# Recurrent-memory attention in a pipelined pair of layers: first step written out with segment 0's values made in place, and one-layer steps with another order and another output projection

## The chip, the core and the metric

The kernel runs on one core of one Trainium2 chip. The core has a matrix engine (TensorE, PE in the profile, with its weight loads as PEld), a vector engine (VectorE, DVE), an activation engine (ScalarE, ACT), GpSimd (POOL), a queue engine that only issues transfers (SyncE, SP), and 16 DMA engines that move data between DRAM and the on-chip memory SBUF. Matrix products are accumulated in PSUM, whose banks are read by DVE and ACT. The metric is the device time of one execution in microseconds (us); lower is better. Times are compared by their median.

## The reference

Four layers follow each other on a sequence of 2048 tokens of width 512 in bf16: attention with a recurrent memory (A), a dense block (B), A again, B again, each behind a layer norm and with a residual. Weights are shared by the two A layers and by the two B layers.

```python
def _A_ref(x, mem0, Wq, Wk, Wv, Wo, seg_len):       # M=8 memory rows, segments of 32 tokens, H=32 heads of 128
    mem = mem0
    for s in range(n_seg):                          # 64 segments, one after the other
        h = jnp.concatenate([mem, xs], axis=1)      # 40 rows: memory, then the segment's tokens
        q, k, v = h @ Wq, h @ Wk, h @ Wv            # per head
        p = softmax(mask(q @ k.T * scale))
        o = (p @ v) @ Wo
        mem = o[:, :M]                              # the memory of the next segment
        outs.append(o[:, M:])
x = x + _A_ref(_layernorm(x), ...); x = x + relu(_layernorm(x) @ w1) @ w2   # w1 512x1376, w2 1376x512
x = x + _A_ref(_layernorm(x), ...); x = x + relu(_layernorm(x) @ w1) @ w2
```

## The kernel before

**Steps.** Segment s+1 needs the memory that segment s leaves, so each A layer is a chain of 64 links. The kernel runs the second A layer four segments behind the first: step k works on segment k of the first layer and segment k-4 of the second. Steps 4 to 63 have both layers; steps 0 to 3 and 64 to 67 have one (`layers(k)` has one entry). The dense block of a position is done two steps later and fills gaps of the chain.

**Order.** PE, DVE, SP and POOL execute in the order in which the code is written. Only ACT's order is chosen by a planner, by priority; `tc.high_priority` marks the work of the chain.

**One step, `step(k)`**, in PE's order: queries and keys of heads 0 to 15 (`qk(0)`, three batches, products L466, copies L470 on ACT and L472 on DVE); the first part of the previous step's token projection (`block`, which calls `output_x(k-1)`, L349 for 32 rows, L328 for 64); `scores` (L496) and `softmax` (L512 to L526); `qk(1)` for heads 16 to 31; hidden layer of the dense block (`dense_h`, L408, ReLU on ACT L411); scores and softmax of heads 16 to 31; the rest of `block`; `dense_y` (L426); `transpose_p(1)` (L534, copies L538); weighted values (`weighted_v`, L560) and their copies (`outputs`, L578); the projection of the memory rows (`output_mem`, L504); its copy `wm` (ACT L740); values of the second layer's next tokens (`values1`, L309); `mt`, which turns `wm` (L753), and its copies to `HT` (DVE L758, memory rows for the next queries and keys) and to `HTm` (ACT L759, memory rows for the next values); `memory_values(k+1)` (L638). `HT` and `HTm` open the next step.

**On DVE** the add of the token projection into the residual, `add_output(k-1)` (L363), is written between the softmax of heads 16 to 31 and `transpose_p(1)`; the add of the dense block, `add_dense` (L334), after `outputs`. Then come `HT`, the norm's moments, the norm and the masks.

**Probabilities** of heads 0 to 15 are transposed by a DMA (`turn_p`, L541, from `P_sb` to `PT0`), except in steps 0, 1 and 67 (`by_pe`), where PE does it. The softmax of heads 16 to 31 writes the same `P_sb`, so it waits for that DMA.

**Values** go through DRAM. `values0(p, n)` makes the first layer's values of two segments (64 tokens; L288) and stores them in `vd0[p]` (L297); `memory_values` makes those of the memory rows and of some later tokens and stores them in `vmd` (L643); `load_values` (L614 to L622) and `load_memory_values` (L648) bring them to `Vs`, whose rows are keys. In step 0 these stores and loads are issued by POOL (`q = nc.gpsimd`), in later steps by SP.

**Banks.** `ps_c` has three PSUM banks (tag "c"), `ps_fill` two, `ps_wo` one. `output_x` and `output_mem` both use `ps_wo`, so `output_mem(k)` cannot start before `add_output(k-1)` has read the bank. SBUF tiles of tag "vst" (five) stage what is stored to DRAM.

**Start.** SP issues the weights in the order Wq, Wk (first halves), Wv, second halves of Wq and Wk, then Wo in four quarters; the dense weights w1 and w2 come in step 1 (`load_dense`, L151 to L154).

Of the kernel before, what the change touches and what calls it, by code (L numbers as in the profile page):

```python
# [7 lines left out]
BF = mybir.dt.bfloat16  # L8
# [14 lines left out]
def kernel(  # L23
# [254 lines left out]
    def values0(p, n, lo=0, hi=NC4, pool=None):  # L278
        r = 64 * (p % 2)
        if (n, lo) == (0, 0):  # L280
            vd0[p] = dram.tile([64, H * Dh], BF, tag="vd0", bufs=3, name="vd0")
        if lo == 0:
            pool, tag = (pool, "wo") if pool else (ps_fill, "fill")
            vp_tiles[p, n] = pool.tile([128, 512], F32, tag=tag, name="vp")
        vp = vp_tiles[p, n]
        for c4 in range(lo, hi):
            for j in range(2):
                nc.tensor.matmul(vp[64 * j:64 * j + 64, :], lhsT=xT0[p // 2][:, c4, r:r + 64],  # L288
                                 rhs=Wv_sb[:, c4, (n + j) * 512:(n + j + 1) * 512],
                                 start=(c4 == 0), stop=(c4 == NC4 - 1), tile_position=(0, 64 * j))  # L290
        if hi < NC4:
            return
        q = nc.sync if p >= 1 else nc.gpsimd
        vst = wk.tile([128, 512], BF, tag="vst", bufs=5)
        nc.scalar.copy(out=vst[:], in_=vp[:])
        for j in range(2):
            q.dma_start(out=vd0[p][:, (n + j) * 512:(n + j + 1) * 512], in_=vst[64 * j:64 * j + 64, :])  # L297

    def values1(s, ii):
        if not has1(s):  # L300
            return
        if ii == 0:
            vd1[s] = dram.tile([2, 4, 32, 512], BF, tag="vd1", bufs=3, name="vd1")
        r = base(s - DELTA)
        vp = ps_fill.tile([128, 512], F32, tag="fill", name="v1")
        for c4 in range(NC4):
            for j in range(4):
                n = 4 * ii + j
                nc.tensor.matmul(vp[32 * j:32 * j + 32, :], lhsT=xnT_tiles[s - 1][:, c4, r:r + SEG],  # L309
                                 rhs=Wv_sb[:, c4, n * 512:(n + 1) * 512],  # L310
                                 start=(c4 == 0), stop=(c4 == NC4 - 1), tile_position=(0, 32 * j))
        vst = wk.tile([128, 512], BF, tag="vst", bufs=5)
        nc.scalar.copy(out=vst[:], in_=vp[:])
        nc.sync.dma_start(out=vd1[s][ii].rearrange("j t e -> (j t) e"), in_=vst[:])
# [22 lines left out]
    def output_x(k, lo, hi):  # L337
        if not 0 <= k <= LAST or ox_span(k) is None:
            return
        r0, r1 = [x % 64 for x in (ox_span(k)[0], ox_span(k)[1] - 1)]  # L340
        r1 += 1
        if lo == 0:
            wo_tiles[k] = ps_wo.tile([128, Dm], F32, tag="wo", name="wox")
        for h in range(lo, hi):
            if r1 - r0 == 64:
                halves(wo_tiles[k], OTx[:, h, r0:r1], Wo_sb[:, h, :], h == 0, h == H - 1)
            else:
                for j in range(4):
                    nc.tensor.matmul(wo_tiles[k][32 * j:32 * j + 32, 0:128], lhsT=OTx[:, h, r0:r1],  # L349
                                     rhs=Wo_sb[:, h, 128 * j:128 * j + 128], start=(h == 0), stop=(h == H - 1),  # L350
                                     tile_position=(0, 32 * j))

    def add_output(k):
        if not 0 <= k <= LAST or ox_span(k) is None:
            return
        r0, r1 = ox_span(k)
        R = residual(k)
        if r1 - r0 == 64:
            add_halves(R[r0:r1, :], R[r0:r1, :], wo_tiles[k])
        else:  # L360
            for j in range(4):
                cs = slice(128 * j, 128 * j + 128)
                nc.vector.tensor_tensor(out=R[r0:r1, cs], in0=R[r0:r1, cs],  # L363
                                        in1=wo_tiles[k][32 * j:32 * j + 32, 0:128], op=ALU.add)
# [246 lines left out]
    def load_values(k, act, q):  # L611
        for a in act:
            if a == 1:
                q.dma_start(out=Vs[64 + M:64 + L, :].rearrange("t (n e) -> t n e", n=NCH),  # L614
                            in_=vd1.pop(k)[:].rearrange("i j t e -> t (i j) e"))
            elif k >= 4 and k % 4 < 2:
                for u in range(2):
                    lo = M + 2 * M * u
                    q.dma_start(out=Vs[lo:lo + 2 * M, :].rearrange("t (n e) -> t n e", n=NCH),
                                in_=vmds[k - k % 4 - 4 + 2 * (k % 4) + u][:, :, 2 * M:32, :].rearrange("i j t e -> t (i j) e"))  # L620
            else:
                q.dma_start(out=Vs[M:L, :], in_=vd0[k // 2][SEG * (k % 2):SEG * (k % 2) + SEG, :])  # L622
# [8 lines left out]
    def memory_values(k, q):  # L631
        vmd = vmds[k] = dram.tile([2, 4, 32, 512], BF, tag="vmd", bufs=7, name="vmd")
        for ii in range(2):
# [7 lines left out]
            VmS = wk.tile([128, 512], BF, tag="vst", bufs=5, name="VmS")  # L641
            nc.scalar.copy(out=VmS[:], in_=vp[:])  # L642
            q.dma_start(out=vmd[ii].rearrange("j t e -> (j t) e"), in_=VmS[:])  # L643

    def load_memory_values(k, act, q):
        for ii in range(2):
            for a in act:
                q.dma_start(out=Vs[64 * a:64 * a + M, 2048 * ii:2048 * (ii + 1)].rearrange("m (j e) -> m j e", j=4),  # L648
                            in_=vmds[k][ii, :, a * M:(a + 1) * M, :].rearrange("j t e -> t j e"))
# [12 lines left out]

    def step(k):
        act = layers(k)
        q = nc.sync if k > 0 else nc.gpsimd
# [3 lines left out]
        by_pe = k in (0, 1, LAST)  # L669
        if k % 4 == 0 and has_x:  # L670
            load_xb(n_x)
        if k == 0:
            masks(*act)
        with tc.high_priority(offset=PRIO):
            qks = qk(0, act)
        if k == 0:
            for n in range(0, NCH, 2):
                values0(0, n)
        with tc.high_priority(offset=PRIO):
            if k == 1:  # L680
                load_values(k, act, q)
            if k < 2:
                memory_values(k, q)
            if k != 1:
                load_values(k, act, q)
        part = 5 if len(act) == 2 else 8
        block(k, 0, part)
        with tc.high_priority(offset=PRIO):
            transpose_step(k)
            load_memory_values(k, act, q)  # L690
            scores(qks, act)
            softmax(0, act, by_pe)
            if not by_pe:
                turn_p()
# [8 lines left out]
        if k < LAST:  # L703
            dense_h(k - 2)
# [3 lines left out]
        block(k, part, H)  # L708
        if k == 0:
            for n in (0, 2):  # L710
                values0(1, n)
        if k == 1:
            values0(1, 6)
        ahead = has1(k + 1) or not cont
# [3 lines left out]
        add_output(k - 1)  # L718
# [9 lines left out]
        with tc.high_priority(offset=PRIO):  # L728
            pvs = weighted_v(act)
            outputs(k, pvs)  # L730
            if cont:
                wo = ps_wo.tile([128, Dm], F32, tag="wo", name="wo")
                if k == 0:
                    output_mem(k, wo, 0, 24)
                    values0(1, 4)
                    output_mem(k, wo, 24)
                else:
                    output_mem(k, wo)
                wm_sb = wm_tiles[k] = wk.tile([128, Dm], BF, tag="vst", bufs=5, name="wm")
                nc.scalar.copy(out=wm_sb[:], in_=wo[:])  # L740
        if not ahead:
            dense_y(k - 2, f_mid, NFC)
        if k < LAST:
            add_dense(k - 2)
            store(k - 2)
        values1(k + 1, 0)
        if cont:
            with tc.high_priority(offset=PRIO):
                c = 1 - k % 2
                mt = ps_c.tile([128, NC4, 2, M], F32, tag="c", name="mt")  # L750
                for c4 in range(NC4):
                    for r in range(0, 128, 32):
                        nc.tensor.matmul(mt[r:r + 32, c4].rearrange("p a m -> p (a m)"),  # L753
                                         lhsT=wm_sb[:, c4 * 128 + r:c4 * 128 + r + 32],
                                         rhs=sel[:, 4 * M * c:4 * M * c + 2 * M], start=True, stop=True,
                                         tile_position=(0, r))
                lo, hi = cont[0], cont[-1] + 1
                nc.vector.tensor_copy(out=HT[:, :, lo:hi, 0:M], in_=mt[:, :, lo:hi, :])  # L758
                nc.scalar.copy(out=HTm[:, :, lo * M:hi * M], in_=mt[:, :, lo:hi, :].rearrange("p c a m -> p c (a m)"))  # L759
        values1(k + 1, 1)  # L760
        if cont:
            output_ride(k)
            with tc.high_priority(offset=PRIO):
                if k > 0:
                    memory_values(k + 1, nc.sync)
        if k < LAST:
            moments(k + 1, True)
        add_ride(k)
        if k < LAST:
            moments(k + 1, False)  # L770
            with tc.high_priority(offset=PRIO):
                normalize_step(k + 1)
# [4 lines left out]
    with tc.manual_schedule(engines={mybir.EngineType.PE, mybir.EngineType.DVE, mybir.EngineType.SP,  # L777
# [14 lines left out]
        for k in range(LAST + 1):  # L792
            step(k)
# [56 lines left out]
```

## Time and profile before

| what | value |
|---|---|
| median of 3 runs | 1621.66 us (1618.75 to 1623.23) |
| the profiled execution: time, span | 1618.67 us, 1617.0 us |
| PE busy in 0 to 40, 40 to 60, 60 to 80, 80 to 100, 100 to 120 us | 16.53, 15.05, 16.55, 16.74, 17.41 us |
| PE busy in 140 to 280 us | 140.00 us |
| PE busy in 1540 to 1560, 1560 to 1580, 1580 to 1600, 1600 to 1617 us | 19.47, 19.14, 18.04, 9.47 us |

Matrix products are pipelined and the profile models their ends, so a PE that is busy throughout is one that always has a product in flight. In an answer of the timeline a row has the start and the length in us, the engine, the line, the operation with output and inputs, the number of instructions, and in brackets how long the engine idled before and what released it; "issue" means that it waited for nothing that the profile shows. The chain of waits is the work that ended last, followed back; a row is start, length, what.

### The profile page before, as it was taken

Reading aid. Unit: us, or ns where it says so; the run is one execution under the profiler, and the core shown is the slowest. Engines: PE = TensorE matmul, PEld = TensorE weight load, DVE = VectorE, ACT = ScalarE, POOL = GpSimd, SP = SyncE. Lnnn points to the kernel's source line nnn. Section 1 sums busy time; section 2 is a strip of 40 time slices with the busy share of each in tenths; the row PEclk is TensorE's granted clock in tenths of the full one; section 3 lists DMA queues with packets and bytes.
Section 4 is the critical chain, followed back from the end, with each engine's and each line's share of the span. In section 5 each row is a group of like instructions: output and inputs, shape, how many; then the busy total and the mean of one; then the engine's idle time right before and its main releaser. Section 6 shows DMA issues by size and latency. Waiting matters only on the chain.

```text
span 1617.0 us, 95434 instructions
## 1 busy us (share of the span) xinstructions
PE 1565.2 (97%) x42998; PEld 1322.3 (82%) x42998; DVE 1257.4 (78%) x3107; ACT 738.3 (46%) x1798; POOL 352.3 (22%) x678
## 2 busy tenths in 40 slices
PE   4789999999999999999999999999999999999997
PEld 2568888988888898889888888888888898888876
DVE  2568888888888887888888888888888888887765
ACT  1334445454444545454454545445444544544442
POOL 4012122222222222222222222222222222221210
PEclk9999999999999999999999999999999999999999
DMA  9634433443444344343344543535344343424321
GB/s 374 199 58 87 85 81 73 92 92 75 84 90 81 77 83 96 79 79 86 82 91 68 99 85 79 77 86 92 64 99 83 76 82 81 94 57 100 69 68 38
DMA packets 216504, 147.15 MB, mean 91 GB/s; under 512 B 125672, under 2 KB 209168, under 8 KB 215008
## 3 DMA queue, kind: packets, MB, share of 16 engines
q1 hardware_dynamic: 212560, 135.74, 39.0%
q8 instruction: 337, 5.52, 1.6%
q0 software_dynamic: 3536, 5.31, 1.4%
q14 instruction: 71, 0.58, 0.1%
HBM read 65.74 MB, written 45.61 MB: 69 GB/s over the span
## 4 chain that ended last, share of the span: by engine, by line
PE 92%; DVE 2%; SPq 2%; DMA 2%; issue 1%; ACT 1%; POOL 0%; POOLq 0%; DVEq 0%; ACTq 0%
PE qp L466 37%; PE wox L328 10%; PE wo L504 8%; PE vm L638 7%; PE v L309 7%; PE hp L408 5%; PE sp L426 5%; PE sp L496 4%; PE pv L560 4%; PE vp L288 3%; SPq L145 1%; PE tp L534 1%; DMA Wo_sb<-in_A_Wo_dram 1%; SPq L134 1%; PE xp L384 1%
## 5 line engine op out<-in xcount | busy, mean ns | idle before, releaser
L470 ACT CAST QT<-qp 128x480 bf16<-128x480 f32 (+3 forms) x408 | 201.5, 494 | 402.1 <-PE qp L466 399.8
L466 PE MATMUL qp<-HT,Wk_sb 128*128 128x80 bf16 (+1 forms) x8704 | 369.8, 200 | 7.7 <-DMA Wk_sb<-in_A_Wk_dram 5.5
L466 PE MATMUL qp<-HT,Wq_sb 128*128 128x80 bf16 (+1 forms) x8704 | 370.8, 200 | 2.5 <-POOL HT L629 1.2
L466 PEld LDWEIGHTS <-Wq_sb 128*128 128x128 bf16 x8704 | 327.0, 100 | 34.1 <-issue 28.0
L466 PEld LDWEIGHTS <-Wk_sb 128*128 128x128 bf16 x8704 | 329.1, 100 | 8.6 <-DMA Wk_sb<-in_A_Wk_dram 5.6
L472 DVE CAST KT<-qp 128x480 bf16<-128x480 f32 (+3 forms) x408 | 225.4, 566 | 107.8 <-PE qp L466 105.9
L526 POOL TENSOR_TENSOR P_sb<-es,sm 128x320 bf16<-128x320 f32 x185 | 131.1, 722 | 767.6 <-DVE sm L524 577.6
L512 DVE TENSOR_REDUCE mx<-sp 128x8 f32<-128x320 f32 x256 | 114.9, 487 | 94.0 <-PE sp L496 92.8
L328 PE MATMUL wox<-Wo_sb,OTx 128*64 128x256 bf16 x2880 | 173.4, 273 | 0.0
L523 DVE TENSOR_REDUCE sm<-es 128x8 f32<-128x320 f32 x256 | 119.0, 465 | 43.2 <-ACT es L518 32.7
L328 PEld LDWEIGHTS <-OTx 128*64 128x64 bf16 x2880 | 150.2, 110 | 2.9
L638 PE MATMUL vm<-Wv_sb,HTm 128*32 128x512 bf16 x2176 | 136.6, 382 | 1.3 <-PE mt L753 1.0
L518 ACT ACTIVATE es<-es 128x320 f32<-128x320 f32 x256 | 110.7, 469 | 54.5 <-DVE es L516 52.9
L504 PE MATMUL wo<-Wo_sb,OTm 128*32 128x512 bf16 x2144 | 129.0, 381 | 3.3 <-DMA Wo_sb<-in_A_Wo_dram 3.2
L309 PE MATMUL v<-Wv_sb,xnT 128*32 128x512 bf16 x2048 | 128.7, 378 | 0.0
L488 DVE CAST sp<-maskb 128x320 f32<-128x320 bf16 x256 | 118.4, 484 | 0.0
L516 DVE TENSOR_TENSOR es<-sp,mx 128x320 f32<-128x320 f32 x256 | 113.7, 483 | 1.5
L638 PEld LDWEIGHTS <-HTm 128*32 128x32 bf16 x2176 | 88.5, 97 | 31.2 <-issue 14.0
L426 PE MATMUL sp<-w_sb,hT 128*64 128x256 bf16 (+4 forms) x1474 | 104.9, 275 | 1.2 <-ACT hT L411 1.2
L642 ACT CAST VmS<-vm 128x512 bf16<-128x512 f32 x136 | 79.7, 586 | 54.3 <-PE vm L638 54.0
L408 PE MATMUL hp<-xnT,w_sb 128*128 128x64 bf16 (+3 forms) x2948 | 100.2, 193 | 0.7 <-ACT xnT L809 0.7
L408 PEld LDWEIGHTS <-w_sb 128*128 128x128 bf16 (+1 forms) x2948 | 94.4, 101 | 0.9 <-issue 0.8
(98 smaller groups left out, 2019.4 us busy)
## 6 DMA issues: line engine op xcount, KB each, us to landing
Vs<-vd SPq DMA_DIRECT2D x97, 256.0 KB
vmd<-VmS SPq DMA_DIRECT2D x134, 128.0 KB
vd<-vst SPq DMA_DIRECT2D x128, 128.0 KB
vd<-vst SPq DMA_DIRECT2D x128, 64.0 KB
Vs<-vmd SPq DMA_DIRECT2D x254, 32.0 KB
Vs<-vmd SPq DMA_DIRECT2D x60, 128.0 KB
Wq_sb<-in_A_Wq_dram SPq DMA_DIRECT2D x2, 2048.0 KB
Wk_sb<-in_A_Wk_dram SPq DMA_DIRECT2D x2, 2048.0 KB
```

What stands on the lines that cost most here:

```text
L309: nc.tensor.matmul(vp[32 * j:32 * j + 32, :], lhsT=xnT_tiles[s - 1][:, c4, r:r + SEG], rhs=Wv_sb[:, c4, n * 512:(n + 1) * 512], start=(c4 ...
L328: nc.tensor.matmul(out[64 * j:64 * j + nr, 0:256], lhsT=lhsT, rhs=rhs[:, 256 * j:256 * j + 256], start=start, stop=stop, tile_position=(0, ...
L408: nc.tensor.matmul(hp[0:fs, fc - f0, 0:n], lhsT=w1_sb[:, c4, fc * 128:fc * 128 + fs], rhs=cols(c4), start=(c4 == 0), stop=(c4 == NC4 - 1))
L426: nc.tensor.matmul(sp_banks[bank][64 * j:64 * j + n, 0:w], lhsT=hT_tiles[d][0:fs, fc, 0:n], rhs=w2_flat[0:fs, fc * Dm + 256 * j:fc * Dm + ...
L466: nc.tensor.matmul(qp[:, hi, 0:ncol], lhsT=W_sb[:, c4, h * Dh:(h + 1) * Dh], rhs=HT[:, c4, a_lo:a_hi, :], start=(c4 == 0), stop=(c4 == NC4 ...
L470: nc.scalar.copy(out=dst[:, 0:nh, a_lo * L:a_hi * L], in_=qp[:, 0:nh, 0:ncol])
L472: nc.vector.tensor_copy(out=dst[:, 0:nh, a_lo * L:a_hi * L], in_=qp[:, 0:nh, 0:ncol])
L488: nc.vector.tensor_copy(out=sp_tiles[a], in_=maskb2)
L504: nc.tensor.matmul(wo[32 * j:32 * j + 32, :], lhsT=OTm[:, h, n, 2 * M * c:2 * M * c + 4 * M], rhs=Wo_sb[:, h, :], start=(h < 4), stop=(h > ...
L523: nc.vector.tensor_reduce(out=sm[:], in_=es[:], axis=AX.X, op=ALU.add)
L526: eng.tensor_tensor(out=P_sb[:, :, 64 * a:64 * a + L], in0=es[:], in1=sm[:].unsqueeze(2).to_broadcast([128, 8, L]), op=ALU.mult)
L638: nc.tensor.matmul(vp[32 * j:32 * j + 32, :], lhsT=HTm[:, c4, :], rhs=Wv_sb[:, c4, n * 512:(n + 1) * 512], start=(c4 == 0), stop=(c4 == NC ...
```

## The change

Four things change.

1. **Step 0 is written out as `first_step()`.** `values_first` multiplies the 40 rows of `HT` (memory and segment 0) with Wv and copies the result straight into `Vs` rows 0 to 39. Segment 1's values are made by `values_second` (same form as `values1`, 32 rows in four column groups), segments 2 and 3 by `values0(1, n)` as before, in pieces between the quarters of `output_mem`. What is stored to DRAM is staged in eight pieces of the still empty `w1_sb`, and all stores go to SP.
2. **One-layer steps:** eight heads of `block` come between `qk(1)` and the scores, `dense_h` behind them, `add_output(k-1)` behind `outputs`, and `output_mem` uses `ps_c`. In both kinds of step `wm`, `values1(k+1, 0)`, `mt` and the two copies are in `new_memory`; in steps 1 and 2 the copy to `HTm` goes to DVE and is written first. In step 2 `add_dense` comes behind `new_memory`.
3. **By heads:** for outputs of 32 rows whose next step has one layer (`by_heads(k)`: k = 1, 2, 64, 65), each of the 32 heads is one product of 512 columns into one of four row groups of the bank, and `add_output` adds the four groups, 512 columns each. Before, a head was four products of 128 columns and each add had 128 columns.
4. The last token projection, `output_x(67)`, uses `ps_c`.

```diff
+    def values_first():
+        for n in range(0, NCH, 2):
+            vp = ps_fill.tile([128, 512], F32, tag="fill", name="vf")
+            for c4 in range(NC4):
+                for j in range(2):
+                    nc.tensor.matmul(vp[64 * j:64 * j + L, :], lhsT=HT[:, c4, 0, :],
+                                     rhs=Wv_sb[:, c4, (n + j) * 512:(n + j + 1) * 512],
...
+            copy = nc.scalar.copy if n % 4 == 0 else nc.vector.tensor_copy
+            for j in range(2):
+                copy(out=Vs[0:L, (n + j) * 512:(n + j + 1) * 512], in_=vp[64 * j:64 * j + L, :])
+    def values_second(stage):
+        vd0[0] = dram.tile([2, 4, 32, 512], BF, tag="vd_second", bufs=1, name="vd_second")
+        for ii in range(2):
+            values_tile(xT0[0][:, :, SEG:2 * SEG], ii, vd0[0], stage[ii])
...
-            wo_tiles[k] = ps_wo.tile([128, Dm], F32, tag="wo", name="wox")
+            pool, tag = (ps_wo, "wo") if k < LAST else (ps_c, "c")
+            wo_tiles[k] = pool.tile([128, Dm], F32, tag=tag, name="wox")
...
+            elif by_heads(k):
+                j = h % 4
+                nc.tensor.matmul(wo_tiles[k][32 * j:32 * j + 32, :], lhsT=OTx[:, h, r0:r1], rhs=Wo_sb[:, h, :],
+                                 start=(h < 4), stop=(h >= H - 4), tile_position=(0, 32 * j))
+    def by_heads(k):
+        return k + 1 < LAST and len(layers(k + 1)) == 1
...
+        if by_heads(k) and r1 - r0 == 32:
+            for j in range(4):
+                nc.vector.tensor_tensor(out=R[r0:r1, :], in0=R[r0:r1, :], in1=wo_tiles[k][32 * j:32 * j + 32, :],
+                                        op=ALU.add)
...
+    def new_memory(k, cont, wo):
+        wm_sb = wm_tiles[k] = wk.tile([128, Dm], BF, tag="vst", bufs=5, name="wm")
+        nc.scalar.copy(out=wm_sb[:], in_=wo[:])
+        values1(k + 1, 0)
...
+        for f in (to_queries, to_values) if k == 0 or has1(k + 1) else (to_values, to_queries):
+            f()
...
+    def first_step():
+        stage = [w1_sb[:, i // 2, 512 * (i % 2):512 * (i % 2) + 512] for i in range(8)]
+        load_xb(2)
+        masks(0)
+        with tc.high_priority(offset=PRIO):
+            qks = qk(0, [0])
+            scores(qks, [0])
+            softmax(0, [0], True)
+            values_first()
+            load_x(1)
+            qks = qk(1, [0])
+            scores(qks, [0])
+            softmax(1, [0], True)
+            memory_values(0, stage[0:2])
+            values_second(stage[2:4])
+            transpose_p(1)
+            tokens_in(1)
+            nc.gpsimd.tensor_copy(out=HTm[:, :, 2 * M:32], in_=spare_T(1))
+            pvs = weighted_v([0])
+            outputs(0, pvs)
+            wo = ps_wo.tile([128, Dm], F32, tag="wo", name="wo")
+            for n in range(0, NCH, 2):
+                output_mem(0, wo, 4 * n, 4 * n + 8)
+                if n < 6:
+                    values0(1, n, stage=stage[4 + n // 2])
+            new_memory(0, [0], wo)
+            output_ride(0)
+            prepare(1)
...
         with tc.high_priority(offset=PRIO):
             qks = qk(1, act)
-        if k < LAST:
+        if single:
+            block(k, part, 16)
+        else:
             dense_h(k - 2)
         with tc.high_priority(offset=PRIO):
             scores(qks, act)
             softmax(1, act, by_pe)
-        block(k, part, H)
+        if single:
+            if k < LAST:
+                dense_h(k - 2)
+            block(k, 16, H)
+            if k == 1:
+                values0(1, 6)
+        else:
+            block(k, part, H)
...
-        add_output(k - 1)
+        if not single:
+            add_output(k - 1)
...
             pvs = weighted_v(act)
             outputs(k, pvs)
+        if single:
+            add_output(k - 1)
+        if cont:
+            with tc.high_priority(offset=PRIO):
+                pool, tag = (ps_c, "c") if single else (ps_wo, "wo")
+                wo = pool.tile([128, Dm], F32, tag=tag, name="wo")
+                output_mem(k, wo)
         if not ahead:
             dense_y(k - 2, f_mid, NFC)
-        if k < LAST:
+        if k < LAST and ahead:
             add_dense(k - 2)
             store(k - 2)
-        values1(k + 1, 0)
         if cont:
             with tc.high_priority(offset=PRIO):
...
+                new_memory(k, cont, wo)
+        if not ahead:
+            add_dense(k - 2)
+            store(k - 2)
         values1(k + 1, 1)
```

## The prediction

> **What bounds it.** I read the page, then busy time by stretches, the chain of waits, and the timeline of both ends. The chain is PE for 92% of the span, and from 140 to 280 us PE is busy throughout. In steps 4 to 63 the order on PE, DVE and SP stays, and ACT's order there (wm, first vst, HTm, second vst) is already what the new priorities ask for: cost nothing, covered by PE itself. What can move lies in the first 120 us and the last 90.
>
> The timeline of the start (start us, length us, instruction, idle before it and its releaser):
>
> ```profile
> 38.62 0.98 PE L466 MATMUL qp<-HT,Wk_sb 128*128 128x40 bf16 x24 [5.53 <-DMA Wk_sb<-in_A_Wk_dram]
> ...
> 45.59 0.48 PE L534 MATMUL tp<-ident,P_sb 128*64 128x80 bf16 x16 [0.87 <-DVE P_sb L526]
> ...
> 47.08 1.05 PE L504 MATMUL wo<-Wo_sb,OTm 128*32 128x512 bf16 x16
> ...
> 53.29 1.04 PE L504 MATMUL wo<-Wo_sb,OTm 128*32 128x512 bf16 x8 [0.87 <-DMA Wo_sb<-in_A_Wo_dram]
> ```
>
> Step 0 waits for Wk's second half and for Wo's last quarter. The stretches (busy PE, PEld, DVE, ACT, POOL; granted clock, DMA share, GB/s) show the transfers busy but slow, and later a half clock:
>
> ```profile
> 34.00:36.00 2.00, 0.00 (x0) 0.00 (x0) 1.10 (x3) 0.00 (x0) 0.00 (x0) 1.00 1.01 399
> 42.00:44.00 2.00, 1.91 (x46) 1.40 (x46) 1.61 (x5) 0.65 (x2) 0.98 (x3) 1.00 0.96 183
> 44.00:46.00 2.00, 1.13 (x25) 0.51 (x20) 1.32 (x4) 1.35 (x4) 0.00 (x0) 1.00 1.19 229
> 56.00:58.00 2.00, 2.00 (x66) 2.00 (x64) 1.30 (x3) 0.36 (x1) 0.00 (x0) 0.50 0.23 86
> ```
>
> **Start: -3.3.** Before 38.6 us POOL's queue moves 512 KB of vd and 256 KB of vmd among the weights; at the measured 0.41 MB/us this is 1.9 us. Staged on SP behind Wo, they no longer precede Wk, which lands near 36.7. From 38.62 to the end of the scores before took 4.1 us, so they end at 40.8. PE then does tp(0) 0.4, memory_values 1.9 and values_second 1.9 (32 products as at L638 and L309): 45.0. The softmax ends 2.85 after the scores (42.69 to 45.53), at 43.6: no wait. tp to the first wo took 1.5 (45.59 to 47.08): 46.5. Then four times 8 heads (32 take 1.84, so 0.46) and three values0 of 8 products (0.96): 51.2; I take 51.0, since tp waited a little for DVE before. The wo before ended at 54.36. Wo: the transfers that shared the queues with it (a 256 KB Vs load into 32 partitions, where the rate falls to 183 and 229 GB/s) are gone; 4.19 MB at 0.34 to 0.41 MB/us from 36.7 land at 47 to 49, before the 50.5 at which the last quarter is needed. If they land at 51.5 instead, the gain is 2.3; with no ACT or bank delay at all it is 4.0. values_first stands where values0(0) stood, with as many products (32, 3.8) under the same wait for Wv: 0, and 3.8 if Wv and Wk came without a wait. memory_values leaves PE's wait for Wk (29.2 to 32) for the path; its 1.9 is in the sum. Stores now stand on SP ahead of step 1's Vs load, but that load has until 66 us and w1's until step 2.
>
> **Clock: -0.7.** Step 1's first 128 products take 3.96 at a granted 0.50, against 3.30 in step 2 at 1.00. In the new step 0 PE has no long gap after 36.7. Between 0 and -0.7.
>
> **One-layer steps.** Step 65 in the chain of waits:
>
> ```profile
> 1555.63 1.35 PE hp L408 x44
> ...
> 1559.70 0.49 DVE P_sb L526
> 1560.19 0.18 DVE R L363
> ...
> 1561.30 0.50 DVE PT_sb L538
> ...
> 1561.84 0.35 PE pv L560 x8
> 1562.20 1.84 PE wo L504 x32
> 1564.04 0.86 PE v L309 x16
> ...
> 1565.87 1.73 PE vm L638 x32
> ```
>
> DVE's four adds delay the second PT_sb copy, which delays pv, then wo. New, from the end of qk(1) = T: 8 heads of wox 0.46, scores 0.32, hp 1.35, 16 heads 0.92, dense_y 1.01, so tp at T+4.1; P_sb, 2.9 after the scores, ends at T+3.7. tp 0.35, dense_y 0.22, pv 0.85: wo at T+5.5, against 6.57: **-1.05**. The 32-row projection by heads has no row; bounds are wox L349 in the tail (128 in 1.97) and wo L504 (32 in 1.84, the same shape), and I take the latter. Its first 8 heads save 0.84 - 0.46 = **0.4** before scores.
>
> Two more changes of PE's array shape per step cost something: 32 wo behind pv take 1.84, 32 v behind each other 1.74; vm behind v 1.73, behind qp 1.84. Between 0 and 0.12 each; I take 0.12, since that row has the same shape: **+0.25**. [...]
>
> The bill comes behind outputs:
>
> ```profile
> 55.82 0.67 DVE L391 TENSOR_TENSOR R<-R,xp 32x512 f32<-32x512 f32 x1 [0.20 <-PE xp L384]
> ...
> 1565.11 0.19 DVE L758 CAST HT<-mt 128x32 bf16<-128x32 f32 x1 [0.97 <-PE mt L753]
> ```
>
> Four adds of 512 columns are 4 x 0.68 = 2.7 (L391 is the row of that shape; 4 x 0.28 = 1.1 each, if the columns of L363 added up, is the upper end; 0.42, L334's 256 columns, the lower). They and add_dense (0.85) stand ahead of HT on DVE; HT had 0.97 of idle before it, so it comes 1.7 later, HTm behind it, and vm, which had some 0.15 to spare, **+1.55**. Queued behind HT are the moments and the norm, which move with vm and are no later against it.
>
> PE's "issue" gaps are where many tiny products run: 0.81 in step 2's qk(1), 0.55 and 0.27 in step 3, 0.32 each in 65 and 66, up to 1.76 in wox L349; step 64, whose wox is 64 products instead of 128, has none. With 32 I expect none either: **-0.32** in 65, the same in 66.
>
> By step, then:
> - 65: -1.05 - 0.4 + 0.25 + 1.55 - 0.32, about 0. 66: tp to wo as in 65, wo 6.71 after T, so -1.2; first heads 0.64 - 0.46; in all +0.1.
> - 64: 64 rows as before and PE-bound; +0.25. Its adds (0.85) fit ahead of HT.
> - 2: P_sb waits for turn_p's DMA, which by the trace's semaphore landings lands at 88.45 (DVE started at 88.85): -0.35, the adds gone -0.55, first heads -0.37. Behind: HTm waits for the adds, 4.15 after wo instead of 3.98, and add_dense, now behind HT, puts the first key copy 0.2 too late for its bank: +0.4. Sum -0.9. Its qk gap moves no DMA landing: 0.
> - 3: turn_p lands 5.3 after issue (110.87) and P_sb waits for it; so -0.6 up to wo, -0.1 first heads, -0.55 for the gap in its first scores, +1.55: +0.3.
> - 1: HTm first, on DVE: vm 74.34 to 74.1, -0.2.
> - 67: adds no longer ahead of PT_sb (1601.0 could be 1600.35): -0.6, shape +0.1: -0.5. The projection's own bank is used where nothing waited for it: 0.
>
> **Sum**: -3.3 - 0.7 - 0.2 - 0.9 + 0.3 + 0.25 + 0 + 0.1 - 0.5 = -4.95, say -4.9. The profiled execution, 1618.67, becomes 1613.8; it lies 3 us under the median of the runs, so the forecast is 1621.66 - 4.9 = **1616.8**. 0.3%, about what a measurement of this kernel can tell from no change, is 4.9 us: the forecast sits on that bound.
>
> **Rivals.**
> - *Wo still lands last, or PE's clock stays low*: the start gives 2.3 and the clock nothing: 1621.66 - 4.9 + 1.7 = 1618.5. For it: 348 GB/s at 46 to 48 us, when mostly Wo moved. Against: 768 KB and the slow load are gone. 20%.
> - [...] 21%.
> - *DVE's queue behind outputs becomes the bound*: adds at 1.1 each are 1.7 us more before HT in steps 2, 3, 65, 66, +6.8: 1623.6, slower than before. For it: L363 too reads PSUM rows other than those it writes, while L391's 0.67 has the same rows; against: 256 columns cost 0.42, far under 0.56. It decides as soon as an add exceeds 0.99 (4.9 over 16 adds, on top of 0.68). 14%.
> - The forecast's own case, 1614.5 to 1619: 45%.
>
> **From these**: faster by over 0.3%: 24 of the forecast's 45, 20 of the gaps case, 2 of Wo's: 0.46. Slower by over 0.3%: 9 of DVE's case, 1 of Wo's: 0.10. Within: 0.44. Range: worst, start 2.3, no clock gain, steps 64 to 67 without gains for gaps: about 1621.5; best, the second rival with 1.5 us more of the stalls hidden: 1612. A planner that puts a ReLU (0.60) ahead of the exponential in the five steps with a dense block would cost up to 3.0 and is covered from 1616.8 up to 1620.
>
> **What would show it.** Start: Wk near 36.7, last wo quarter not waiting for DMA, wo's end near 51, clock 1.00 in step 1's qk. Steps 3, 65, 66: DVE add rows of about 0.68, HT right behind add_dense, PE idle some 1.5 before vm with HTm as releaser; no issue gaps in L349 except steps 4 and 67 and the tail. Wrong would be: a Wo wait before wo's end, steps 4 to 63 of another length, adds near 1.1, or vm of 65 not waiting.

## The result and the profile after

The changed kernel takes 1624.38 us in the median of 22 runs (1619.34 to 1631.34), the kernel before 1621.45 in as many (1617.76 to 1624.10): a ratio of 1.002, 95% interval [1.0011, 1.003]. It is slower by a little, where 4.9 us of gain were forecast. The profiled execution of after has a time of 1621.61 us and a span of 1619.9, 2.9 more than before's 1617.0. That this is also the difference of the medians is luck: the runs of after spread over 12 us, and their time goes with the mean granted clock of the run (0.988 to 0.994, correlation -0.76). The ledger below is made of the two profiles, one execution each.

A step is counted from its first query product (L498, L466 before) to that of the next step. What a single profile can carry is seen in steps 4 to 63, which are written the same in all kernels of this study: in the other profiles they take from 3.9 us less (e5 below) to 0.8 more (e10) than in before's, and 3.5 more in e6.

| part | predicted | profiles (after less before) |
|---|---|---|
| step 0 and start | -3.3 | -0.39 |
| step 1 (clock -0.7, copies -0.2) | -0.9 | +0.40 |
| step 2 | -0.9 | -0.78 |
| step 3 | +0.3 | -0.06 |
| steps 4 to 63 | 0 | +0.84 |
| step 64 | +0.25 | +1.12 |
| step 65 | 0 | +0.36 |
| step 66 | +0.1 | +1.00 |
| step 67 and tail | -0.5 | +0.41 |
| sum | -4.95 | +2.90 |

The timeline of PE at the start, after:

```profile
37.09 0.98 PE L498 MATMUL qp<-HT,Wk_sb 128*128 128x40 bf16 x24 [4.28 <-DMA Wk_sb<-in_A_Wk_dram]
...
41.77 0.39 PE L670 MATMUL vm<-Wv_sb,HTm 128*32 128x512 bf16 x1
43.70 1.91 PE L670 MATMUL vm<-Wv_sb,HTm 128*32 128x512 bf16 x31 [1.54 <-issue]
45.23 2.10 PE L329 MATMUL v<-Wv_sb,xT 128*32 128x512 bf16 x32
47.27 0.48 PE L566 MATMUL tp<-ident,P_sb 128*64 128x80 bf16 x16
...
48.83 0.61 PE L536 MATMUL wo<-Wo_sb,OTm 128*32 128x512 bf16 x8
49.38 1.05 PE L288 MATMUL vp<-Wv_sb,xT 128*64 128x512 bf16 x8
...
54.73 0.27 PE L703 MATMUL mt<-sel,wm 128*32 128x16 bf16 x16 [0.69 <-ACT wm L697]
```

Wk comes 1.5 us earlier than before's 38.62, and no output product waits for Wo. But behind the first product of `memory_values` PE stands still for 1.54 us without a releaser, and tp is 1.7 later than before's 45.59. Each round of 8 output products and one piece of `values0` takes 0.55 + 0.98.

Three of the stretches of time that were shown of before, and two more (columns as there; the granted clock is the third number from the end):

```profile
38.00:40.00 2.00, 2.00 (x66) 2.00 (x63) 0.69 (x2) 0.36 (x1) 0.00 (x0) 0.50 1.10 349
42.00:44.00 2.00, 0.46 (x9) 0.19 (x12) 1.79 (x5) 0.63 (x2) 0.00 (x0) 1.00 1.10 351
44.00:46.00 2.00, 2.00 (x44) 1.01 (x40) 0.26 (x1) 0.93 (x2) 0.32 (x2) 1.00 1.10 348
56.00:58.00 2.00, 2.00 (x87) 2.00 (x84) 0.82 (x3) 0.72 (x2) 0.00 (x0) 1.00 0.55 154
70.00:74.00 4.00, 3.31 (x49) 1.15 (x48) 1.02 (x3) 0.67 (x2) 0.17 (x1) 0.71 1.08 363
```

The slow transfers of 42 to 46 us are gone (351 and 348 GB/s instead of 183 and 229), and step 1's first products have the full clock: the spell of half clock from 51.5 to 58.4 us is gone. The one on the keys and queries at 38 us was there before too (37.9 to 41.3; now 27.9 to 41.6). New is one on step 1's output products, from 68.9 to 72.3.

The chain of waits in step 65, after:

```profile
1557.05 1.45 PE hp L440 x44
...
1561.81 0.22 PE pv L592 x8
...
1562.28 0.80 DVE OTx L610 x2
1563.08 0.59 DVE R L388
...
1565.12 0.69 DVE R L388
...
1566.25 0.42 DVE R L354
...
1566.71 0.20 DVE HT L714
...
1566.93 0.20 ACT HTm L711
...
1567.17 1.91 PE vm L670 x32
```

Before, the chain ran over PE from wo to vm. Now it leaves PE behind pv and runs through six adds on DVE up to vm.

### The profile page after: what moved, and what is told of

It is laid out like the page before. It is cut to its first block, busy times and chain, and to the rows that moved or that the text cites. A ratio compares the mean times of both kernels' runs of the same rounds, so it can differ in the third digit from the quotient of the medians.

```text
span 1619.9 us, 94712 instructions
## 1 busy us (share of the span) xinstructions
PE 1567.9 (97%) x42646; PEld 1318.8 (81%) x42646; DVE 1266.6 (78%) x3113; ACT 739.0 (46%) x1798; POOL 346.9 (21%) x665
## 3 DMA queue, kind: packets, MB, share of 16 engines
q8 instruction: 334, 5.47, 1.6%
## 4 chain that ended last, share of the span: by engine, by line
PE 92%; DVE 3%; DMA 3%; issue 1%; ACT 1%; SPq 1%; POOL 0%; POOLq 0%; DVEq 0%; ACTq 0%
PE qp L498 37%; PE wox L348 10%; PE wo L536 7%; PE vm L670 7%; PE v L329 7%; PE hp L440 5%; PE sp L458 5%; PE pv L592 4%; PE sp L528 4%; PE vp L288 3%; DMA Wk_sb<-in_A_Wk_dram 2%; PE tp L566 1%; DMA PT<-P_sb 1%; PE xp L416 1%; SPq L134 0%
## 5 line engine op out<-in xcount | busy, mean ns | idle before, releaser
L498 PE MATMUL qp<-HT,Wk_sb 128*128 128x80 bf16 (+1 forms) x8704 | 370.0, 200 | 6.7 <-DMA Wk_sb<-in_A_Wk_dram 4.3
L498 PE MATMUL qp<-HT,Wq_sb 128*128 128x80 bf16 (+1 forms) x8704 | 370.3, 200 | 5.1 <-DMA Wq_sb<-in_A_Wq_dram 2.7
L498 PEld LDWEIGHTS <-Wq_sb 128*128 128x128 bf16 x8704 | 326.7, 100 | 37.1 <-issue 27.4
L498 PEld LDWEIGHTS <-Wk_sb 128*128 128x128 bf16 x8704 | 329.3, 100 | 7.9 <-DMA Wk_sb<-in_A_Wk_dram 4.4
L504 DVE CAST KT<-qp 128x480 bf16<-128x480 f32 (+3 forms) x408 | 225.2, 565 | 108.7 <-PE qp L498 106.9
```

The costliest lines, as they stand in the source:

```text
L498: nc.tensor.matmul(qp[:, hi, 0:ncol], lhsT=W_sb[:, c4, h * Dh:(h + 1) * Dh], rhs=HT[:, c4, a_lo:a_hi, :], start=(c4 == 0), stop=(c4 == NC4 ...
L504: nc.vector.tensor_copy(out=dst[:, 0:nh, a_lo * L:a_hi * L], in_=qp[:, 0:nh, 0:ncol])
```

## The experiments

All ratios are to the kernel before on the same chip. Runs made together share one set of runs of it.

### Taking the change apart

Theory: the added stall behind outputs (the adds by heads ahead of `HT`) and the start, which won nothing, together make the loss; the new order by itself gains. Rival: scattered gaps and clock, not tied to any part.

`e1_start_only` keeps `first_step()` and has the one-layer steps of before. `e2_steps_only` is the reverse. `e3_no_heads` is the changed kernel without outputs by heads:

```diff
     def by_heads(k):
-        return k + 1 < LAST and len(layers(k + 1)) == 1
+        return False
```

`e5_order_only` is e2 with that edit too.

> The written-out first step alone; the one-layer steps are those of before. If the one-layer steps are what makes the changed kernel slower (their memory copies wait behind the adds on VectorE: 1.6 us more from mt to vm in steps 3, 65 and 66), this one is at or under before: ratio 0.998 to 1.000, and mt to vm is 1.0 there. If the start is the cause (memory_values stalls 1.5 us on the way, half clock until 41.6 us), it is slower than before by 1 to 2 us, and step 1's first product comes no earlier than 55.3.

> The one-layer steps of the changed kernel behind the first step of before. If the one-layer steps are the cause: 1 to 3 us slower than before, ratio 1.001 to 1.002, with 2.6 us from mt to vm in steps 3, 65, 66 instead of 1.0. If the start is the cause: ratio 0.999 to 1.000.

> The changed kernel with outputs of 32 rows made and added as before (four products of 128 columns for a head, adds of 128 columns); the new order stays. If the four adds of 512 columns ahead of the memory copies are what costs, mt to vm falls from 2.6-2.8 to about 1.2 us in steps 3, 65 and 66, and the time falls by 3 to 5 us against the changed kernel: ratio to before 0.998 to 0.9995. If it is the place of the adds and not their length, mt to vm stays over 2 and the ratio stays 1.001 to 1.003.

> Start of before; the one-layer steps have the new order (projection in its own bank, outputs 16 + 16 heads around the dense layer, adds behind the projection), but the 32-row outputs stay in column quarters, added in four pieces of 128. Theory (the four 512-wide adds ahead of the memory copies are all that the one-layer steps lost): the step from mt to vm is back at 1.0 us in steps 3, 65 and 66, steps 2, 3, 65 and 66 together come out some 2.5 us shorter than before, ratio 0.998 to 0.999. Rival (the new order itself gains nothing, what the profile showed there was clock and instruction gaps): the four steps within 0.5 us of before, ratio 0.9995 to 1.0005.

| one-layer steps | start of before | start of after |
|---|---|---|
| of before | 1 | 1.0012 [1.0001, 1.0023] |
| new order, no heads | 0.9989 [0.9977, 1.0] | 1.0000 [0.9988, 1.0013] |
| new order, by heads | 1.0017 [1.0004, 1.0031] | 1.002 [1.0011, 1.003] |

Down each column the new order takes 0.11 to 0.12% off and the outputs by heads put 0.20 to 0.28% on; across, the start puts on 0.03 to 0.12%. Only for the outputs by heads behind the old start are the two intervals clear of each other; for the new order and the start the ratios alone do not decide. The profiles point the same way. Steps 2, 3, 65 and 66 together take 82.2 us in the mean of before and e1 (two profiles), 80.5 without heads (six profiles of this study, 79.0 to 82.7), and 84.0 with heads (four, 83.6 to 84.4; e6 below is left out). That is -1.7 and +3.4 us, or -0.10% and +0.21%; the second is clear of the scatter, the first is not (before 83.0, e1 81.3). From mt to vm steps 3, 65 and 66 take 2.66, 2.62 and 2.78 us in after and 1.00, 0.97 and 1.12 in e3. Step 1's first product comes at 55.71, 55.66 and 55.37 with the old start (before, e2, e5) and at 55.32, 56.58, 57.12 and 58.25 with the new one (after, e1, e3, and e6 below): 1.2 us later in the mean, though with the same code it lies anywhere in 2.9 us. So the start wins nothing, and by e1's interval it loses a little; the 0.39 us that the one profile of after wins are not typical. The theory holds for the outputs by heads and for a start without gain; its rival fails on steps 3, 65 and 66. e3's ratio missed its expected 0.998 to 0.9995 by a little.

### Is it the place of the adds, or their length?

`e6_memory_first` keeps the outputs by heads, and issues all adds behind the copies of the memory:

```diff
-        if single:
+        if single and not cont:
             add_output(k - 1)
...
-        if k < LAST and ahead:
+        if k < LAST and ahead and not single:
             add_dense(k - 2)
             store(k - 2)
...
                 new_memory(k, cont, wo)
+        if single and cont:
+            add_output(k - 1)
+        if not ahead or (single and k < LAST):
+            add_dense(k - 2)
...
```

> The changed kernel with its 32-row outputs by heads, but in the one-layer steps the adds into the residual (four of 512 columns at 0.69 us and the two of the dense layer at 0.42) are issued behind the copies of the new memory, which then stand first in VectorE's queue. Theory of place: from mt to vm 1.0 us instead of 1.62 to 1.81 more, in steps 3, 65 and 66, and nothing else late because the 64 products of memory_values cover the 3.6 us of adds; ratio 1.000 to 1.001 where the changed kernel had 1.002. Rival of length: VectorE is as busy as before, so the 3.6 us appear one place later, as a wait of the next step's products for the copies of K; from q0 to T the steps after 3, 65 and 66 are 1 us or more longer, ratio 1.0015 to 1.0025.

Measured: 1.0041 [1.0026, 1.0055], worse than the changed kernel. From mt to vm it takes 1.00, 0.98 and 0.97 us, as the theory of place has it, but the next step's products grow longer (first to last query or key product: step 4 from 10.26 to 11.96, step 65 from 7.40 to 8.64, step 66 from 7.41 to 10.17, in which 0.8 is a half clock). The timeline of e6 at the end of step 65 and in step 66 (DVE and PE):

```profile
1570.73 2.81 DVE L388 TENSOR_TENSOR R<-R,wox 32x512 f32<-32x512 f32 x4
...
1571.21 1.90 PE L670 MATMUL vm<-Wv_sb,HTm 128*32 128x512 bf16 x32
...
1578.10 0.95 DVE L504 CAST KT<-qp 128x240 bf16<-128x240 f32 x3
1578.56 0.81 PE L528 MATMUL sp<-KT,QT 128*40 128x40 bf16 x16 [0.96 <-DVE KT L504]
```

vm is in time. But adds, statistics, masks and norm now keep DVE from 1570.7 to 1578.1, and all three key copies come behind them; the scores wait 0.96. In steps 3, 4, 65 and 67 the trace has such waits for L504 of 1.75, 1.53, 1.08 and 1.33. The rival of length is right about the wait: DVE has no 2.8 us to spare here. Its ratio, 1.0015 to 1.0025, was exceeded, and not all of the excess is the move: the start, which the edit leaves alone, is 2.9 us longer in this profile than in after's, and the mean granted clock of the runs is 0.990 against 0.9925. PE wins nothing from the outputs by heads: 8 heads take 0.61 by heads (L370, 8 products) and 0.63 in quarters (L374, 32 products).

### Where the start lost its gain

`e4_values_early` is the changed kernel with two lines moved, so that PE does this work while it waits for Wk:

```diff
             load_x(1)
+            memory_values(0, stage[0:2])
+            values_second(stage[2:4])
             qks = qk(1, [0])
             scores(qks, [0])
             softmax(1, [0], True)
-            memory_values(0, stage[0:2])
-            values_second(stage[2:4])
             transpose_p(1)
```

`e7_early_no_heads` is e3 with that edit. `e8_fill_wait` is e7 with the three pieces of `values0(1, n)` moved ahead of `transpose_p(1)`, where PE still waits for the softmax. `e11_shift_block` leaves the changed kernel's order and adds 100 products of 128x40 to PE behind `values_first()`.

> The changed kernel with memory_values(0) and values_second ahead of qk(1), in TensorE's wait for Wq and Wk, instead of behind the scores. If these 64 products on the path and the instruction stall inside them are what took the start's gain, the transposes of step 0 start near 44 us instead of 47.3 and step 1's first product near 52 instead of 55.3; the time falls by 3 us against the changed kernel (ratio to before 1.000). If Wo or the stores bind step 0 anyway, step 1 starts at 55 and the ratio stays 1.002.

> The changed kernel without outputs by heads, and with memory_values(0) and values_second ahead of the queries and keys of step 1, so that they run while Wk's last part and the copies are on their way. Theory (the start lost its gain because this work stood on the path behind softmax): first product of tp(0) at 44 to 45 us instead of 47.27, first query product of step 1 at 53 to 54 instead of 55.32, ratio 0.998 to 0.999. Rival (the start is set by clock and instruction blocks that fall anew in every run): q0 of step 1 at 55 to 57, ratio 0.9995 to 1.0005.

> As the run with early values and no outputs by heads, but the three values0 pieces of the first step stand between softmax(1) and transpose_p(1), where TensorE waits for the softmax, instead of between the quarters of the output; the 32 output products run in one piece. Theory (the alternation cost about 1.5 us a round, and the wait before tp is long enough to hold the pieces): tp(0) at 44 to 45.5, from the first wo to mt 4 to 5 us instead of 7, first query product of step 1 at 51 to 52.5, ratio 0.997 to 0.998. Rival (the wait is too short, the pieces delay tp by as much as they are shorter in the output): tp(0) at 47, q0 of step 1 as in the run without this move, ratio equal to it within 0.0005.

> The changed kernel, with 100 products of 128x40 into a bank that nothing reads behind the first values, where TensorE waits for Wq and Wk (extra work, output unchanged). They put some 200 instructions ahead of everything that follows on TensorE. Theory (the stop of 1.5 to 1.8 us behind the first product of memory_values, seen at the same product in all four kernels with this start, is TensorE waiting for its next block of 256 instructions; the packet ends 1.3 to 1.8 us before the product): the block's boundary moves into the wait for Wk, memory_values runs as 32 products in one piece, first product of tp(0) at 45 to 46 instead of 47.27, first query product of step 1 at 53 to 54.3 instead of 55.32, ratio 1.0005 to 1.0015. Rival (the stop belongs to that place: the bank, the weights' transfers or the mask): it stays behind the first product of memory_values at 1.3 us or more, tp(0) at 47 or later, ratio 1.002 or above.

| kernel | ratio | first tp(0) us | first query product of step 1, us |
|---|---|---|---|
| after | 1.002 [1.0011, 1.003] | 47.27 | 55.32 |
| e4 | 1.0017 [1.0003, 1.003] | 44.35 | 53.59 |
| e11 | 1.0000 [0.9989, 1.001] | 46.26 | 54.32 |
| e3 | 1.0000 [0.9988, 1.0013] | 49.06 | 57.12 |
| e7 | 0.9984 [0.9971, 0.9997] | 44.51 | 55.20 |
| e8 | 0.9965 [0.9953, 0.9977] | 44.04 | 51.41 |

e8 is faster than both kernels, by 0.35% against before; its interval is clear of e3's. e4 and e7 win 1.7 and 1.9 us at the end of step 0 in the profile (against after and e3), but their medians do not show it beyond their intervals: e4's ratio is where its rival had it, not at the 1.000 of its theory. e7's own expectation for step 1 (53 to 54) was missed, because the half clock lay on its output products at 46 us (wo 1.04, values0 1.92 for 8 products each).

e11 is about the stop. In the trace, a packet of 16384 bytes of PE's instructions (some 256 of them, by the count: after has 334 such packets, 5.47 MB in all, for some 85,700 instructions on PE and PEld) is fetched just then:

```
kernel   packet, us        vm product 1   vm product 2
after    40.99 to 42.07    41.77          43.70
e1       40.87 to 42.01    41.15          43.36
e3       41.22 to 42.36    41.55          43.85
e6       41.27 to 42.42    41.82          43.77
e11      32.82 to 33.90    41.87          no stop
         41.58 to 42.75
```

The stop is at the same product in all four kernels with this start, and it ends 1.35 to 1.63 us behind the end of the packet. It is not the only one: in the thirteen profiles PE has 99 idle stretches of over 0.15 us (from 25 us on, those in front of a later vm left out) whose releaser is "issue", and every one ends 1.0 to 1.75 us behind the end of such a packet. With 200 instructions (products and their weight loads) put ahead, one packet falls into the wait for Wk. The next one, from 41.58, is fetched while `memory_values` runs and stops nothing, so a fetch alone is not a stop. The timeline of e11 has no stop:

```profile
29.05 2.65 PE L760 MATMUL busy<-Wv_sb,ident 128*128 128x40 bf16 x100 [0.41 <-ACT Vs L309]
...
37.07 0.98 PE L498 MATMUL qp<-HT,Wk_sb 128*128 128x40 bf16 x24 [4.44 <-DMA Wk_sb<-in_A_Wk_dram]
...
41.87 2.73 PE L670 MATMUL vm<-Wv_sb,HTm 128*32 128x512 bf16 x32
44.22 2.11 PE L329 MATMUL v<-Wv_sb,xT 128*32 128x512 bf16 x32
46.26 0.48 PE L566 MATMUL tp<-ident,P_sb 128*64 128x80 bf16 x16
```

More work on PE, and the ratio is 1.0000 where after had 1.002. The gain is above the 1.0005 to 1.0015 expected, tp and step 1 are 0.3 and 0.02 later than expected; the profile's span is 4.6 shorter than after's, of which 1.0 is the start and 1.2 step 1's half clock, which did not come in this run; the rest is scattered. So the edit shows that the stop goes with the packet and not with the place, but its ratio is not the stop's price: the added products also keep PE busy, and the mean granted clock over all runs is 0.9961 in e11 and 0.9925 in after. The two are not separated here.

PE in e8, for comparison:

```profile
41.22 3.02 PE L288 MATMUL vp<-Wv_sb,xT 128*64 128x512 bf16 x24
44.04 0.48 PE L566 MATMUL tp<-ident,P_sb 128*64 128x80 bf16 x16
...
45.73 1.48 PE L536 MATMUL wo<-Wo_sb,OTm 128*32 128x512 bf16 x24
49.47 0.62 PE L536 MATMUL wo<-Wo_sb,OTm 128*32 128x512 bf16 x8 [2.26 <-DMA Wo_sb<-in_A_Wo_dram]
...
67.56 3.32 PE L536 MATMUL wo<-Wo_sb,OTm 128*32 128x512 bf16 x32
```

The pieces fit into the softmax wait, the output comes in one piece, and now it is Wo's last quarter that the start waits for. Step 1's output products still take 3.32 instead of 1.91.

### What brings the half clock

`e9_busy_one` adds 8 products of 128x512 that nothing reads to e8, in step 1's wait for the softmax. `e10_busy_two` puts `values0(1, 6)` and 5 such products into the wait for Wo, and 12 into step 1's wait.

```diff
+    def busy(n):
+        d = ps_fill.tile([128, 512], F32, tag="fill", name="busy")
+        for i in range(n):
+            nc.tensor.matmul(d[:], lhsT=ident[:], rhs=Wv_sb[:, 0, 0:512], start=(i == 0), stop=(i == n - 1))
...
             if k == 1:
                 values0(1, 6)
+                busy(8)
```

> As the run with the values0 pieces in the softmax wait, plus 8 products of 128x512 into a bank that nothing reads, in step 1's wait for the softmax (there TensorE was busy 0.26 of 2.00 us). Extra work, output unchanged. Theory (that idle stretch is what brings the half clock to step 1's output products): from the first wo of step 1 to mt 2.6 us instead of 4.01, no half-clock window between 60 and 80 us, ratio 0.9955 to 0.996. Rival (the window is answered by idle time elsewhere, or the added products delay tp by as much): W to mt stays at 3.6 to 4.0, or T to tp grows from 3.72 by 1 us or more; ratio 0.9965 to 0.997.

> As the run with the values0 pieces in the softmax wait, with the fourth values0 piece of step 1 and 5 products of 128x512 into a bank that nothing reads placed ahead of the last 8 output products of step 0, where TensorE waited 2.26 us for Wo's last part, and 12 such products in step 1's softmax wait. Extra work, output unchanged. Theory (idle stretches bring the half clock about 2 to 8 us later): no half-clock window from 48 to 80 us, step 1 from q0 to T 9.1 instead of 10.67 and from wo to mt 2.6 instead of 4.01, step 1 in all 19.7 instead of 22.68, ratio 0.9945 to 0.9955. Rival (filling them changes only where the windows fall, and the added products go late themselves): step 1 at 21 us or more, ratio 0.9965 or above.

The stretch of step 1's wait and of its output products, e8:

```profile
64.00:66.00 2.00, 0.26 (x13) 0.20 (x12) 1.79 (x5) 0.93 (x2) 0.00 (x0) 1.00 0.96 312
68.00:70.00 2.00, 2.00 (x24) 0.77 (x20) 0.69 (x2) 0.00 (x0) 0.00 (x0) 0.50 1.07 374
```

And e9, from its timeline:

```profile
62.06 1.90 PE L758 MATMUL busy<-Wv_sb,ident 128*128 128x512 bf16 x8
63.89 0.48 PE L566 MATMUL tp<-ident,P_sb 128*64 128x80 bf16 x16
...
65.55 1.91 PE L536 MATMUL wo<-Wo_sb,OTm 128*32 128x512 bf16 x32
```

With the wait filled the output products take 1.91, step 1 takes 19.64 in e9 and 19.63 in e10 instead of 22.68, and no half clock lies between 43 and 1590 us in either. (Of e8's 22.68 only 1.4 are the output products; a spell from 50.0 to 56.8, behind its wait for Wo, slowed the queries too. It did not come in e9, where that wait, 1.21, was left empty.) This agrees with the theory for step 1's wait, but two profiles do not show it: the same wait, 1.73 to 1.74 us long, stands unfilled in the other eleven profiles, and in four of them (before, e2, e4 and e11) no half clock followed.

What sets the four apart can be read from the granted clock, whose changes lie on a grid of 3.413 us in each run (in after they come at 27.92, 41.58, 68.88, 72.30, 1604.88, 1608.29 and 1618.53 us, which are 4, 8, 1, 449, 1 and 3 such steps apart). In after, e1, e3, e7 and e8 the whole wait fell into one stretch of this grid, PE was busy for 0.48 to 0.49 of that stretch, and the next one had the half clock, five times of five. In the other six the grid cut the wait, the emptier stretch was busy for 0.58 to 0.65, and the half clock followed in two (e5, e6). In e9 and e10 the stretches with the filled wait are busy for 0.93 to 0.95. Counted from the start of the span, the grid lies 0.3 us past a whole step in before, 0.6 in after, 0.8 in e4 and 2.2 in e1; with the wait filled, no stretch as empty as those five was left there in e9 or e10.

The ratios do not show a gain: 0.9975 [0.9965, 0.9986] and 0.9962 [0.995, 0.9975] against e8's 0.9965, and the three intervals overlap. Nor does the mean granted clock over all runs for step 1's wait alone: 0.9947 in e8, 0.9950 in e9, and 0.9964 in e10 (five runs). That a filled wait is worth time in the median isn't shown.

## Why the prediction was wrong

Of the 7.9 us between the -4.95 of the sum and the +2.90 of the profiles, 2.9 are the start, 1.3 step 1, 2.1 steps 64 to 66, 0.9 the tail and 0.8 steps 4 to 63. T below is the start of the last key product of `qk(1)`.

**Start, -3.3: the step that failed.** Wk near 36.7 (37.09) and no wait for Wo were right. The sum behind them was not; the last output product ends at about 54.0 (mt starts at 54.73 after 0.69 of idle) instead of 51.0. The 3 us: scores end at 41.4 instead of 40.8, for Wk came 0.4 later than taken and the half clock held until 41.6; the stop in `memory_values`, 1.54; `values_second` 2.1 for 1.9; and four rounds of 0.55 + 0.98 where 0.46 + 0.96 were taken, and 0.2 had been taken off besides. The sum allowed PE no stop without a releaser here, though before's trace had such gaps elsewhere (1.76 in step 3's wox). The 1.9 for `memory_values`, which left the wait for Wk, was priced, but not asked about: e4, e7 and e8 show that the wait could have kept it.

**Clock, -0.7: right in its place, undone in the next.** Step 1's queries and keys fell from 9.76 to 9.11, as predicted, and vm came 0.18 sooner after mt by the copies (-0.2 forecast). From wo to mt it rose from 2.60 to 3.76, since the half clock came back at 68.9. "No long gap" was asked of step 0 alone, not of step 1's softmax wait. In e2, e4 and e11, which have the same step 1, it did not come back there and the step takes 19.64, 0.83 less than before: this part of the ledger is the luck of one run.

**Stall behind outputs, +1.55: right.** 1.62, 1.65 and 1.81 in steps 3, 65 and 66, by adds of 0.69 (0.68 taken). The rival with adds at 1.1 is out. What the prediction didn't do is add up its terms for the outputs by heads alone: 1.55 three times and 0.4 in step 2, against first heads (1.05), gaps (1.2) and about 0.3 in the later heads, make a loss of some 2.5 us at its own prices; the profiles have 3.4.

**Steps 2 and 3: right in size** (-0.78 for -0.9, -0.06 for +0.3). In step 3 part of that is chance: T to wo fell by 1.54 where 1.15 was summed, and before's wox there held a pause of 1.76.

**Ahead of wo, -1.05: too large.** In step 65, T to wo fell from 6.68 to 5.93, by 0.75, where -1.05, the gap's -0.32 and the shapes' +0.25 were summed; tp came at T+4.42 instead of T+4.1. From the first query product to T step 65 won 0.56 (0.4 taken), but not by the form of the product: from the first product to what follows, 8 heads take 0.55 by heads (0.46 taken) and 0.56 in quarters, in before's step 3 and in steps 3, 65 and 66 of e3 and e9. Before's 0.84 in step 65 held a pause of 0.28, which the price took for work.

**Shape changes, +0.25: right** where it can be read alone: in step 64 T to tp goes from 5.31 to 5.53, and it is 5.53 in all other kernels with the new order and 5.31 in e1, which has the old one. The sum holds 0.85 for this term (steps 64 to 67), since the author let the 0.12, an estimate from rows of 1.84, 1.74 and 1.73 us, recur at every change. No run shows that it does, nor the 1.4 that the best end of the range, 1612, takes off for it; what the runs show is the 0.22 of step 64.

**Issue gaps, -0.32 each: wrong as a rule.** They left wox in steps 3 and 65 and came up elsewhere, in step 64's keys (0.52 of idle) and step 66's wox (0.25). Fewer products moved the gaps here and did not remove them. That is most of step 64's +1.12: in e3 and e6 to e10, without a pause there, it is +0.2. Of the +0.84 in steps 4 to 63, which no part of the change explains, such pauses make 0.34 (1.13 us of idle against 0.79); 34 of those 60 steps agree within 0.1 us.

**Step 66: a wait that was left out.** `P_sb` waits there for `turn_p`'s DMA, which the prediction counted in steps 2 and 3 alone. DVE in after:

```profile
1580.93 0.49 DVE L558 TENSOR_TENSOR P_sb<-es,sm 128x320 bf16<-128x320 f32 x1 [0.53 <-DMA PT<-P_sb]
```

e2 and e11 have no pause in step 66's wox and wait longer for the DMA instead, 1.21 and 1.19; T to wo is 6.58 in after, 6.63 in e2 and 6.60 in e11, where about 5.5 was forecast. So the order's gain ahead of wo is held there by the DMA, with the pause or without.

**Step 67, -0.5:** T to the output products of the tail fell from 6.45 to 6.13. The adds left `PT_sb`'s way, but only the first product of the second tp came earlier (T+2.61, before T+3.39); the other 15 waited 1.11 for `P_sb`. Then the tail's output products met a half clock (L374, 3.07 instead of 1.97).

**The range.** The terms named for its worst end (start 1.0 less, clock 0.7, gaps 0.64) make 1619.1 of 1616.8, not 1621.5.

## What to carry over

Work that leaves a wait for a transfer should be asked which wait it goes to; here two moved lines and three pieces put into the softmax wait, with the outputs by heads left out, turned +0.2% into -0.35%. A product that needed fewer instructions but left its sum to another engine's adds was no gain here, where that engine opens the next step (mt to vm 2.66 us in step 3 instead of 1.00): moved behind, the same adds made other products wait (0.96 to 1.75 us for the key copies in e6). A price read from a row should be looked at for pauses inside it before a gain is built on it. And a sum of stages on TensorE in a start of many small products needs an allowance for stops without a releaser and for the clock, in this kernel of 1.5 us a time (1.54 in `memory_values`) and 1.1 us (the tail's output products, 3.07 instead of 1.97).

## What the hardware showed

- TensorE stopped 1.34 to 1.91 us (1.34 in e6, 1.54 in after, 1.82 in e1, 1.91 in e3) in `memory_values`, and each stop ended 1.35 to 1.63 us behind the end of a packet of some 256 of its instructions, while weights kept the DMA engines busy (share 1.10 at 42 to 44 us in after), and no longer at that place when 200 instructions were put ahead of it (e11, 32 products in one piece from 41.87).
- The granted clock was 0.5 or 1.0, and every change in a run lay on one grid of 3.413 us, in all thirteen profiles. In before the changes come at 27.64, 31.05, 37.88, 41.29, 51.53, 58.36 and 1614.84 us; the spells of half clock in before and after are one, two and four steps of the grid long (3.41, 6.83 and 13.66 us; the last of a run ends with it). In e8 PE idled from 64.1 to 65.8 us and the half clock began at 67.0, on dense work; where it falls differs between the profiles (from 28.1, 38.3 and 45.1 us in e4; from 26.1, 33.0, 43.2 and 70.5 in e1).
